# A decode attention kernel's output projection: four column tiles with an fp32 sum, and two of A's wo rows a partition loaded apart on 32 partitions

## The chip, the core and the metric

The kernel runs on one core of one Trainium2 chip. A core has TensorE (PE; its weight loads are listed as PEld), VectorE (DVE), ScalarE (ACT), GpSimd (POOL), and SyncE (SP), which here only issues DMAs; 16 DMA engines carry the transfers between HBM and the on-chip memory SBUF. Matmuls write to PSUM, which has banks of 512 fp32 columns. The metric is the device time of one execution in microseconds, as the median of several runs.

## What is computed

Two independent single-token attention layers, A and B, whose output rows are put side by side:

```python
# for A; B is the same with the last W = 4096 keys of its cache
B, Sq, D = 1, 1, 512;  Hq, Hkv, Sk, Dh = 32, 32, 16384, 128
q = (x @ wq).reshape(B, Sq, Hq, Dh).transpose(0, 2, 1, 3)
scores = einsum("bhqd,bhkd->bhqk", q, k_cache) * Dh ** -0.5
p = softmax(scores)
o = einsum("bhqk,bhkd->bhqd", p, v_cache)
row = o.transpose(0, 2, 1, 3).reshape(B, Sq, Hq * Dh) @ wo      # wo: 4096 x 512
out = concatenate([row_A, row_B], axis=-1)                       # 1 x 1 x 1024, bf16
```

All inputs are bf16. A's caches are 128 MB each for K and V, of B's the last quarter is read (32 MB each), and each wo is 4 MB.

## The kernel before

**The main loop.** The work is cut into 20 loads, 16 of A (two heads each) and 4 of B (eight heads each, as two units), one of B after every four of A; the last load is B's. A load is a K tile and a V tile of 128 partitions x 256 keys x 128. For each load, DVE multiplies K by the query (`_mult`, L169) and adds the halves (`_add`, L178); TensorE sums the rest with an identity (`_red`, L190) into the PSUM tile `red`; DVE reduces that to scores (L206) and ScalarE takes the exponential (L212), a load later than the multiplication. `_pv` (L231) multiplies the probabilities with V, with the matmuls spread over four column tiles of TensorE (output rows 0, 32, 64 and 96 in turn, `r = 32 * (t % 4)`); `_fin_pick` (L245, L251) and `_fin_fold` (L259) gather the head's rows into `f_ps`.

**Buffers and the order of DMAs.** K tiles take turns in two buffers (pool `kt`), V tiles have one (pool `vt`). `_Loads` holds a list of transfers with the pool that each needs; `release` frees a slot when the last reader of a tile has been issued, and `pump` then issues what is next in the list, so the order on SP's queue is the list's. The last V tile goes into the `kt` slot of the K tile before the last. After it comes wo, in the one `vt` slot: A's in two pieces of 16 rows a partition, B's in five of 16, 8, 4, 2 and 2 rows a partition (`_load_wo`, L146). wo lies in SBUF with 32 rows a partition, `src = st.wo.rearrange("(p j) f -> p j f", j=J)`, J = 32, so a piece is one run of 16, 8, 4 or 2 KB in each of the 128 partitions.

**The end.** `_fin_rows` sums the exponentials with one fp32 matmul for A and one for B (L270), normalizes (L276, L278) into `orow` (head x 128) and moves `orow` with four small matmuls a layer (L287) to the layout of wo, 128 partitions x 32 columns. `_out` is called once for each piece of wo in the order of the transfers: it copies that tile to bf16 (L300) and multiplies one column of it with one row a partition of wo at a time (L307), 1 x 512 for A (32 matmuls into one PSUM row) and two of 1 x 256 in two column tiles for B (64 matmuls). With the last piece the row is cast to bf16 (L316, L318) and written out by a DMA from SP (L319). The two result rows share one buffer (pool `accs`).

Everything in `_out`, `_fin_rows` and the loads is kept in program order on each engine by `cx.o`.

Of the kernel before, what the change touches and what calls it, by code (L numbers as in the profile page):

```python
# [8 lines left out]
F32 = mybir.dt.float32  # L9
BF16 = mybir.dt.bfloat16  # L10
P = 128
# [3 lines left out]

DH = 128
W = 8
KEYS = 256
SCALE = 1.0 / math.sqrt(DH)

# [119 lines left out]
def _load_wo(nc, cx, st, j0, n):  # L140
    J = st.wo.shape[0] // P
    if cx.wo_t is None:
        cx.wo_t = cx.vt_pool.tile([P, 2, J, st.DN], BF16, tag="vt", name="wo_t")
    src = st.wo.rearrange("(p j) f -> p j f", j=J)
    st.wo_t = cx.wo_t[:, st.at // st.DN, :, :]
    cx.o(nc.sync.dma_start(out=st.wo_t[:, j0 : j0 + n, :], in_=src[:, j0 : j0 + n, :]))  # L146


def _load_kv(nc, cx, load, which, tag):
    pool = cx.kt_pool if tag == "kt" else cx.vt_pool  # L150
    t = pool.tile([P, KEYS, DH], BF16, tag=tag, name=which)
    setattr(load, which, t)
    load.v_tag = tag
    st = load.st
    view = st.k_view if which == "kt" else st.v_view
    for u in load.units:
        src = view[u.h0 : u.h0 + u.R].rearrange("g (i l) d -> i g l d", l=st.keys)
        cx.o(nc.sync.dma_start(out=t[:, u.k0 : u.k0 + st.keys, :], in_=src))
# [42 lines left out]
def _softmax(nc, cx, load):  # L201

    st = load.st
    R = st.R
    sc = cx.sc_pool.tile([P, KEYS], F32, tag="sc", name="sc")
    cx.o(nc.vector.tensor_reduce(out=sc[:, :], in_=load.red[:, :, :], axis=AX.X, op=ALU.add))  # L206
    for u in load.units:
        n = st.keys
        u.p = cx.p_pool.tile([P, n // 4, R, 4], BF16, tag="p", name="p_sb")
        for g in range(R):  # L210
            h = st.f_at + u.h0 + g
            cx.o(nc.scalar.activation(  # L212
                out=u.p[:, :, g, :],
                in_=sc[:, u.k0 : u.k0 + n].rearrange("p (t e) -> p t e", e=4),
                func=ACT.Exp,
                scale=SCALE,
                bias=st.off[:, g : g + 1],
                accum_out=cx.cs[:, h : h + 1],
            ))
# [46 lines left out]

def _fin_rows(nc, cx, sts):
    H = 32
    for st in sts:
        cx.o(nc.tensor.matmul(  # L270
            cx.f_ps[st.f_at : st.f_at + H, DH : DH + 1],
            lhsT=cx.cs[:, st.f_at : st.f_at + H], rhs=cx.ones_col[:, 0:1],
            start=False, stop=True, skip_group_check=True,
        ))
    recip = cx.small.tile([2 * H, 1], F32, tag="recip", name="recip")
    cx.o(nc.vector.reciprocal(recip[:, :], cx.f_ps[0 : 2 * H, DH : DH + 1]))  # L276
    orow = cx.small.tile([2 * H, DH], BF16, tag="orow", name="orow")
    cx.o(nc.scalar.activation(  # L278
        out=orow[:, :], in_=cx.f_ps[0 : 2 * H, 0:DH], func=ACT.Copy, scale=recip[:, 0:1]
    ))  # L280
    for st in sts:
        J = st.wo.shape[0] // P
        n = DH // J
        h = st.f_at
        for r in range(n):
            at = cx.place_at + n * h - r
            cx.o(nc.tensor.matmul(  # L287
                st.oc_ps[:, 0:J],
                lhsT=cx.place[h : h + H, at : at + P],
                rhs=orow[h : h + H, r * J : (r + 1) * J],  # L290
                start=(r == 0), stop=(r == n - 1),
                skip_group_check=True,
            ))


def _out(nc, cx, st, j0, n):
    J = st.wo.shape[0] // P
    if j0 == 0:
        st.oc = cx.singles.tile([P, J], BF16, tag=f"oc{st.name}", name=f"oc{st.name}")
        cx.o(nc.vector.tensor_copy(st.oc[:, :], st.oc_ps[:, 0:J]))  # L300
    if cx.out_ps is None:
        cx.out_ps = cx.red_pool.tile([P, 2, 512], F32, tag="red", name="out_ps")
    w = st.DN // st.cols
    out = [cx.out_ps[r : r + 1, b, 0:w] for r, b in st.out_at]
    for j in range(j0, j0 + n):
        for x in range(st.cols):
            cx.o(nc.tensor.matmul(  # L307
                out[x],
                lhsT=st.oc[:, j : j + 1],
                rhs=st.wo_t[:, j, x * w : (x + 1) * w],  # L310
                start=(j == 0),
                stop=(j == J - 1),
            ))
    if j0 + n == J:
        row = cx.accs_pool.tile([1, st.DN], BF16, tag="accs", name=f"row{st.name}")
        cx.o(nc.vector.tensor_copy(row[0:1, 0:w], out[0]))  # L316
        if st.cols == 2:
            cx.o(nc.scalar.copy(row[0:1, w:], out[1]))  # L318
        cx.o(nc.sync.dma_start(out=cx.out[0, 0:1, st.at : st.at + st.DN], in_=row[0:1, :]))  # L319
# [3 lines left out]
def kernel(  # L323
# [14 lines left out]
    nc = tc.nc  # L338
# [4 lines left out]
    cx = _Ctx()  # L343
# [18 lines left out]
    ld = cx.loads = _Loads({"kt": 1, "vt": 1})  # L362
    cx.scr = cx.kt_pool.tile([P, KEYS * DH], BF16, tag="kt", name="scr")
    cx.wo_t = None

    def problem(name, x, k_cache, v_cache, wq, wo, sk0, W, at):
        st = _Problem()
        st.name, st.x, st.wq, st.wo, st.at = name, x, wq, wo, at
        st.R, st.keys = (2, KEYS) if name == "A" else (4, KEYS // 2)
        assert st.R * W == P * st.keys  # L370
        st.DN = wo.shape[1]
        st.k_view = k_cache[0, :, sk0 : sk0 + W, :]
        st.v_view = v_cache[0, :, sk0 : sk0 + W, :]
        st.out_at = ((0, 0),) if name == "A" else ((64, 0), (96, 1))
        st.cols = len(st.out_at)
        st.f_at = 0 if name == "A" else 32
        assert k_cache.shape[1] == 32
        n = KEYS // st.keys * st.R
        st.loads = [_Load(st, i) for i in range(k_cache.shape[1] // n)]
        st.units = [u for x in st.loads for u in x.units]  # L380
        return st

    stA = problem("A", A_x, A_k_cache, A_v_cache, A_wq, A_wo, 0, SkA, 0)
# [14 lines left out]
            ld.add("vt", lambda x=loads[i - 1]: _load_kv(nc, cx, x, "vt", "vt"))  # L398
    ld.add("kt", lambda x=loads[-1]: _load_kv(nc, cx, x, "vt", "kt"))
    J = A_wo.shape[0] // P  # L400
    pieces = [(stA, 0, J // 2), (stA, J // 2, J // 2)]
    j0 = 0
    for x in (J // 2, J // 4, J // 8, J // 16, J // 16):
        pieces.append((stB, j0, x))
        j0 += x
    for i, p in enumerate(pieces):
        ld.add(None if i else "vt", lambda p=p: _load_wo(nc, cx, *p))

    ld.pump()

# [2 lines left out]
    at = (stA.R + stB.R) * (A_wq.shape[0] // P) * P  # L413
# [9 lines left out]
        out=cx.ident[:, :],  # L423
        in_=ones[:, 0:P],
# [9 lines left out]
    w = cx.place_at + 2 * P  # L434
    cx.place = cx.singles.tile([64, w], BF16, tag="place", name="place")
    nc.gpsimd.affine_select(
        out=cx.place[:, :],
        in_=ones[0:64, 0:w],
# [4 lines left out]
        channel_multiplier=-n_r,  # L443
    )

    cx.cs = cx.singles.tile([P, 64], F32, tag="cs", name="cs")
    rows = cx.small.tile([P, 32], F32, tag="rows", name="rows")
    nc.vector.tensor_reduce(
        out=rows[:, :], in_=cx.ident[:, :].rearrange("p (c w) -> p w c", w=32), axis=AX.X, op=ALU.add,
    )  # L450
    for st in (stA, stB):
        H, R = 32, st.R
# [30 lines left out]
    cx.f_ps = cx.psf_pool.tile([P, 512], F32, tag="f", name="f_ps")  # L483
    stA.oc_ps = cx.pst_pool.tile([P, 512], F32, tag="ocp", name="oc_ps")
    stB.oc_ps = cx.acc[1]
    cx.out_ps = None

    _spread_x(nc, cx, stA, 0, 0)
    _spread_x(nc, cx, stB, 1, stA.R * (A_wq.shape[0] // P) * P)
# [12 lines left out]
    for i, x in enumerate(loads):  # L502
# [11 lines left out]
            end(prev)  # L514
        prev = x
    _softmax(nc, cx, prev)
    for u in prev.units:
        _pv(nc, cx, u)
    end(prev)
# [33 lines left out]
```

The softmax here doesn't subtract the row's maximum and nothing guards it: scores larger than these inputs give would overflow.

## Time and profile before

| what | value |
|---|---|
| median of 4 runs | 823.15 us (822.99 to 823.37) |
| the profiled execution's own time | 823.08 us |
| its span, first to last instruction | 821.4 us |
| mean granted TensorE clock | 0.697 of full |
| DMA | 352.63 MB, mean 429 GB/s over the span |
| busy: DVE / PE / PEld / ACT / POOL | 600.7 / 301.0 / 117.2 / 35.1 / 1.3 us |
| chain that ended last, by engine | DMA 61%, issue 15%, DVE 13%, PE 11% |

All times within a profile are microseconds from the span's start. In tables of groups a line gives the kernel's line, the engine, the operation and the tile, out<-in, with the number of instructions, and in brackets the idle time of the engine before it with what ended it. "DMA" and "GB/s" are the mean busy share of the 16 DMA engines and what they moved. "q1" is the queue row of SP's transfers, "q8" that of instruction fetches, in packets of 16 KB. PEclk is the granted share of the full TensorE clock.

### The profile page before, as it was taken

How to read it: one execution, taken by the hardware profiler on the slowest of the kernel's cores; microseconds unless marked ns; L12 is line 12 of the kernel's file. 1: busy time of each engine (PE TensorE's matmuls, PEld its weight loads, DVE VectorE, ACT ScalarE, POOL GpSimd, SP SyncE). 2: the span in 40 equal slices, each digit the busy share in tenths (PEclk: the TensorE clock that was granted, in tenths of full speed). 3: DMA queues.
4: the chain of work that ended last, by engine and by line, in shares of the span. 5: the costliest groups of instructions: out<-in, count | busy, mean ns of one | idle time of the engine just before them, and what ended most of it. 6: DMA issues, size and time to landing. Idle time of an engine off the chain costs nothing.

```text
span 821.4 us, 4767 instructions
## 1 busy us (share of the span) xinstructions
PE 301.0 (37%) x2148; PEld 117.2 (14%) x2148; DVE 600.7 (73%) x146; ACT 35.1 (4%) x133; POOL 1.3 (0%) x9
## 2 busy tenths in 40 slices
PE   3423705143333415060606151423414250606087
PEld 1211202011111102020202020101101020202033
DVE  2099895996496867799196949599659677689921
ACT  0100000000010000000001000000001000000010
POOL 0000000000000000000000000000000000000000
PEclk9855769585757667686858595857666675758589
DMA  9999999999999999999999999999999999999997
GB/s 385 436 457 412 453 415 451 412 454 418 429 440 447 422 444 426 440 417 448 419 444 437 434 432 437 428 424 441 444 415 451 424 448 418 451 412 450 415 426 317
DMA packets 8236, 352.63 MB, mean 429 GB/s; under 512 B 916, under 2 KB 920, under 8 KB 1304
## 3 DMA queue, kind: packets, MB, share of 16 engines
q1 hardware_dynamic: 8212, 352.33, 99.3%
q8 instruction: 17, 0.28, 0.1%
q14 instruction: 3, 0.02, 0.0%
q10 hardware_dynamic: 4, 0.00, 0.0%
HBM read 352.32 MB, written 0.00 MB: 429 GB/s over the span
## 4 chain that ended last, share of the span: by engine, by line
DMA 61%; issue 15%; DVE 13%; PE 11%; ACT 0%; SPq 0%; DVEq 0%
DMA kt<-in_A_k_cache_dram 42%; DMA vt<-in_A_v_cache_dram 12%; PE red L190 7%; DVE kt L178 6%; DVE kt L169 4%; PE acc L231 4%; DMA vt<-in_B_v_cache_dram 4%; DMA wo_t<-in_B_wo_dram 4%; DVE sc L206 2%; ACT p_sb L212 0%; SPq L115 0%; PE out_ps L307 0%; DVE rowB L316 0%; DVEq L169 0%
## 5 line engine op out<-in xcount | busy, mean ns | idle before, releaser
L169 DVE TENSOR_TENSOR kt<-kt,qallA 128x32768 bf16<-128x32768 bf16 (+2 forms) x20 | 276.2, 13810 | 161.9 <-DMA kt<-in_A_k_cache_dram 161.9
L231 PE MATMUL acc<-vt,p_sb 128*8 128x512 bf16 (+1 forms) x1280 | 113.3, 531 | 443.4 <-ACT p_sb L212 344.1
L178 DVE TENSOR_TENSOR kt<-kt 128x16384 bf16<-128x16384 bf16 (+2 forms) x24 | 174.3, 7262 | 0.2
L190 PE MATMUL red<-kt,ident 128*128 128x512 bf16 x640 | 149.9, 393 | 56.3 <-DVE kt L178 56.3
L231 PEld LDWEIGHTS <-p_sb 128*8 128x8 bf16 (+1 forms) x1280 | 37.7, 112 | 514.9 <-ACT p_sb L212 419.3
L190 PEld LDWEIGHTS <-ident 128*128 128x128 bf16 x640 | 62.6, 100 | 143.0 <-issue 45.3
L169 DVE TENSOR_TENSOR kt<-kt,qallB 128x16384 bf16<-128x16384 bf16 x8 | 69.5, 8686 | 2.7 <-DMA kt<-in_B_k_cache_dram 2.7
L206 DVE TENSOR_REDUCE sc<-red 128x256 f32<-128x2048 f32 x20 | 45.7, 2284 | 5.6 <-PE red L190 5.6
L212 ACT ACTIVATE p_sb<-sc,offA 128x256 bf16<-128x256 f32 x32 | 16.0, 500 | 573.6 <-DVE sc L206 573.6
L245 DVE TENSOR_TENSOR acc<-acc,maskA 128x512 f32<-128x512 f32 x16 | 11.1, 695 | 22.1 <-PE acc L231 22.1
L130 PE MATMUL q_ps<-wq_t,scr 128*128 128x512 bf16 x64 | 17.1, 434 | 6.9 <-DMA wq_t<-in_A_wq_dram 5.0
L212 ACT ACTIVATE p_sb<-sc,offB 128x128 bf16<-128x128 f32 x32 | 12.4, 388 | 160.8 <-DVE sc L206 160.8
L251 DVE TENSOR_REDUCE s<-acc 128x128 f32<-128x512 f32 x24 | 16.6, 692 | 0.8
L245 DVE TENSOR_TENSOR acc<-acc,maskB 128x512 f32<-128x512 f32 x8 | 5.5, 693 | 5.7 <-PE acc L231 5.7
L130 PEld LDWEIGHTS <-scr 128*128 128x128 bf16 x64 | 6.9, 108 | 16.7 <-issue 11.2
L307 PE MATMUL out_ps<-wo_t,ocA 128*1 128x512 bf16 x32 | 8.4, 429 | 0.2 <-DVE ocA L300 0.2
L316 DVE CAST rowA<-out_ps 1x512 bf16<-1x512 f32 x1 | 0.7, 678 | 8.5 <-PE out_ps L307 8.5
L259 PE MATMUL f_ps<-s,selA 128*32 128x128 f32 x32 | 6.5, 285 | 0.0
L212 ACT ACTIVATION_READ_ACCUMULATOR p_sb<-sc,offA 128x1 f32 x32 | 6.0, 187 | 0.0
L212 ACT ACTIVATION_READ_ACCUMULATOR p_sb<-sc,offB 128x1 f32 x32 | 6.0, 186 | 0.0
L102 DVE CAST scr<-xT 128x128 bf16<-128x128 f32 (+1 forms) x6 | 2.1, 460 | 3.6 <-PE xT L94 3.5
L307 PE MATMUL out_ps<-wo_t,ocB 128*1 128x256 bf16 x64 | 4.1, 272 | 1.3 <-DVE ocB L300 0.9
(43 smaller groups left out, 26.4 us busy)
## 6 DMA issues: line engine op xcount, KB each, us to landing
kt<-in_B_k_cache_dram SPq DMA_DIRECT2D x8, 4096.0 KB, 32.8
vt<-in_B_v_cache_dram SPq DMA_DIRECT2D x8, 4096.0 KB, 23.1
wq_t<-in_A_wq_dram SPq DMA_DIRECT2D x1, 4096.0 KB, 12.2
wq_t<-in_B_wq_dram SPq DMA_DIRECT2D x1, 4096.0 KB
wo_t<-in_A_wo_dram SPq DMA_DIRECT2D x2, 2048.0 KB, 22.9
wo_t<-in_B_wo_dram SPq DMA_DIRECT2D x1, 2048.0 KB, 27.3
wo_t<-in_B_wo_dram SPq DMA_DIRECT2D x1, 1024.0 KB, 29.3
wo_t<-in_B_wo_dram SPq DMA_DIRECT2D x1, 512.0 KB
```

Of the source, the lines that this page charges most:

```text
L102: cx.o(nc.vector.tensor_copy(st.xb[:, :, g, :].rearrange("p c (i r) -> p r c i", r=R)[:, g, :, :], xT[:, :].rearrange("p (c o) -> p c o", ...
L130: cx.o(nc.tensor.matmul(q_ps[:, j, :], lhsT=st.xb[:, c, g, :], rhs=w[:, g, j * (512 // DH) : (j + 1) * (512 // DH), :], start=(g == 0 and ...
L169: cx.o(nc.vector.tensor_tensor(out=k, in0=k, in1=q.rearrange("p (o d) -> p o d", o=1).broadcast_to([P, b - a, DH]), op=ALU.mult,))
L178: cx.o(nc.vector.tensor_tensor(out=k[:, :, 0 : DH // 2], in0=k[:, :, 0 : DH // 2], in1=k[:, :, DH // 2 : DH], op=ALU.add,))
L190: cx.o(nc.tensor.matmul(load.red[:, k : k + n, :], lhsT=cx.ident[:, :], rhs=load.kt[:, k : k + n, b * W : (b + 1) * W], start=(b == 0), st ...
L206: cx.o(nc.vector.tensor_reduce(out=sc[:, :], in_=load.red[:, :, :], axis=AX.X, op=ALU.add))
L212: cx.o(nc.scalar.activation(out=u.p[:, :, g, :], in_=sc[:, u.k0 : u.k0 + n].rearrange("p (t e) -> p t e", e=4), func=ACT.Exp, scale=SCALE, ...
L231: cx.o(nc.tensor.matmul(u.acc[r : r + 4 * R, :], lhsT=u.p[:, t, :, :], rhs=u.load.vt[:, k : k + 4, :], start=(t < 4), stop=(t >= T - 4),))
L245: cx.o(nc.vector.tensor_tensor(out=acc, in0=acc, in1=st.mask[:, :].rearrange("p (x o) -> p x o", o=1).broadcast_to([P, 4, DH]), op=ALU.mult,))
L251: cx.o(nc.vector.tensor_reduce(out=u.s[:, :], in_=acc.rearrange("p x d -> p d x"), axis=AX.X, op=ALU.add,))
L259: cx.o(nc.tensor.matmul(cx.f_ps[st.f_at : st.f_at + 32, 0:DH], lhsT=st.sel[:, at : at + 32], rhs=u.s[:, :], start=(u.i == 0), stop=(u.i == ...
L307: cx.o(nc.tensor.matmul(out[x], lhsT=st.oc[:, j : j + 1], rhs=st.wo_t[:, j, x * w : (x + 1) * w], start=(j == 0), stop=(j == J - 1),))
```

## The change

1. A's wo piece of the last rows has 14 rows a partition instead of 16 (`APART = 2`). The two rows left out of each partition, 256 KB, are loaded by `_load_apart` into a tile `more` in the `kt` pool: one partition a head (a block), with 4 x 2 rows of 512 in it, heads 0 to 19 on partitions 0 to 19 and heads 20 to 31 on partitions 32 to 43. Each of its eight DMAs takes every fourth partition, five blocks in the first four DMAs and three in the last four. The first four stand in the list after A's first piece of wo, the last four after A's second. GpSimd sets partitions 0 to 31 of the tile to zero before the first of them.
2. A small matmul with `spread` (a selection of the identity) and a copy bring the values of `orow` that belong to those rows to the same partitions (`oc_x`); they give eight more matmuls of 44 partitions.
3. All of A's matmuls of `_out` (16 + 8 + 14) and B's first 16 (now 1 x 512) go to four column tiles in turn, in one PSUM bank for each layer, which DVE sets to zero after the last softmax. DVE then copies the bank to SBUF as fp32 (`sums`), and an fp32 matmul with a column of ones adds its rows up: for A into a row of another bank, for B into the two 1 x 256 rows after the next eight wo rows a partition (`sum_at` 24).
4. The sums of the exponentials of A and B are one fp32 matmul instead of two, and the bf16 copies of both layers' tiles move from `_out` to `_fin_rows`.

```diff
+APART = 2
+def _load_apart(nc, cx, st, part):
+    J = st.wo.shape[0] // P
+    H = st.wo.shape[0] // DH
+    n = DH // J
+    if part == 0:
+        more = cx.kt_pool.tile([P, KEYS, DH], BF16, tag="kt", name="more").rearrange("p k d -> p (k d)")
+        at = n * APART * st.DN
+        cx.wo_x = more[:, 0:at].rearrange("p (r j f) -> p r j f", r=n, j=APART)
+        cx.sums = more[:, at : at + 2048].bitcast(F32).rearrange("p (b f) -> p b f", b=2)
+        cx.o(nc.gpsimd.memset(cx.wo_x[0:32], 0.0))
+    src = st.wo.rearrange("(h r j) f -> h r j f", h=H, j=J)
+    h0, to, k = ((0, 0, 5), (20, 32, 3))[part]
+    for a in range(4):
+        cx.o(nc.sync.dma_start(
+            out=cx.wo_x[to + a : to + a + 4 * k - 3 : 4],
+            in_=src[h0 + a : h0 + a + 4 * k - 3 : 4, :, J - APART : J, :],
+        ))
 def _fin_rows(nc, cx, sts):
-    for st in sts:
-        cx.o(nc.tensor.matmul(
-            cx.f_ps[st.f_at : st.f_at + H, DH : DH + 1],
-            lhsT=cx.cs[:, st.f_at : st.f_at + H], rhs=cx.ones_col[:, 0:1], ...
+    cx.o(nc.tensor.matmul(
+        cx.f_ps[0 : 2 * H, DH : DH + 1], lhsT=cx.cs[:, :], rhs=cx.ones_col[:, 0:1], ...
...
+        if st.apart:
+            moved = cx.out_ps[0:64, 3, 0 : n * st.apart]
+            cx.o(nc.tensor.matmul(
+                moved, lhsT=cx.spread[:, :],
+                rhs=orow[h : h + H, :].rearrange("p (r j) -> p r j", j=J)[:, :, J - st.apart : J], ...
+            st.oc_x = cx.small.tile([64, n * st.apart], BF16, tag="oc_x", name="oc_x")
+            cx.o(nc.vector.tensor_copy(st.oc_x[:, :], moved))
...
+        st.oc = cx.singles.tile([P, J], BF16, tag=f"oc{st.name}", name=f"oc{st.name}")
+        cx.o(nc.vector.tensor_copy(st.oc[:, :], st.oc_ps[:, 0:J]))
 def _out(nc, cx, st, j0, n):
...
-    for j in range(j0, j0 + n):
+    todo = [(st.oc[:, j : j + 1], st.wo_t[:, j, :]) for j in range(j0, j0 + n)]
+    if st.apart and j0 == 0:
+        todo += [
+            (st.oc_x[0:44, i : i + 1], cx.wo_x[0:44, i // st.apart, i % st.apart, :])
+            for i in range(DH // J * st.apart)
+        ]
+    last = j0 + n == J - st.apart
+    if j0 < st.parts:
+        for i, (oc, wo) in enumerate(todo):
+            r = 32 * (i % 4)
+            cx.o(nc.tensor.matmul(
+                cx.out_ps[r : r + 1, st.bank, :], lhsT=oc, rhs=wo, ...
+        if j0 + n == st.parts:
+            cx.o(nc.vector.tensor_copy(cx.sums[:, st.bank, :], cx.out_ps[:, st.bank, :]))
+        todo = []
+    for i, (oc, wo) in enumerate(todo):
         for x in range(st.cols):
             cx.o(nc.tensor.matmul(
-                out[x], lhsT=st.oc[:, j : j + 1], rhs=st.wo_t[:, j, x * w : (x + 1) * w], ...
+                out[x], lhsT=oc, rhs=wo[:, x * w : (x + 1) * w], ...
+    if j0 + n == st.sum_at:
+        for x in range(st.cols):
+            cx.o(nc.tensor.matmul(
+                out[x], lhsT=cx.ones_col[:, 0:1], rhs=cx.sums[:, st.bank, x * w : (x + 1) * w], ...
-    if j0 + n == J:
+    if last:
...
-        st.out_at = ((0, 0),) if name == "A" else ((64, 0), (96, 1))
+        st.out_at = ((0, 2),) if name == "A" else ((64, 0), (96, 3))
+        st.apart = APART if name == "A" else 0
+        st.bank, st.parts, st.sum_at = (0, 32 - APART, 32 - APART) if name == "A" else (1, 16, 24)
...
-    pieces = [(stA, 0, J // 2), (stA, J // 2, J // 2)]
+    pieces = [(stA, 0, J // 2), (stA, J // 2, J // 2 - APART)]
...
         ld.add(None if i else "vt", lambda p=p: _load_wo(nc, cx, *p))
+        if i < 2:
+            ld.add(None if i else "kt", lambda i=i: _load_apart(nc, cx, stA, i))
...
+    cx.spread = cx.singles.tile([32, 64], BF16, tag="spread", name="spread")
+    nc.vector.memset(cx.spread[:, :], 0.0)
+    nc.vector.tensor_copy(cx.spread[:, 0:20], cx.ident[0:32, 0:20])
+    nc.vector.tensor_copy(cx.spread[:, 32:44], cx.ident[0:32, 20:32])
...
     _softmax(nc, cx, prev)
+    cx.out_ps = cx.red_pool.tile([P, 4, 512], F32, tag="red", name="out_ps")
+    cx.o(nc.vector.memset(cx.out_ps[:, 0:2, :], 0.0))
```

## The prediction, made before the changed kernel had run

> **What bounds the kernel now.** I read the page first: the DMA row and the queues.
>
> ```profile
> DMA  9999999999999999999999999999999999999997
> ...
> q1 hardware_dynamic: 8212, 352.33, 99.3%
> q8 instruction: 17, 0.28, 0.1%
> ```
>
> The 16 DMA engines are busy in every slice but the last: the kernel is a stream of 352 MB, and nothing in the diff changes how many bytes are read. Only the tail can move, so next comes the chain that ended last, in order of time (start us, us, what):
>
> ```profile
> 789.17 29.14 DMA wo_t<-in_B_wo_dram
> 818.31 0.04 issue
> 818.35 0.43 PE out_ps L307 x4
> 818.78 0.41 DVE rowB L316
> ```
>
> The last 256 KB of B's wo lands at 818.31, four matmuls and a cast follow, then the row's DMA. The third view is the busy time by stage over the tail, whose last two columns are the DMA share and GB/s:
>
> ```profile
> 814.00:815.00 1.00, 0.85 (x16) 0.70 (x18) 0.09 (x1) 0.00 (x0) 0.00 (x0) 1.00 0.94 380
> 815.00:816.00 1.00, 1.00 (x22) 0.79 (x18) 0.00 (x0) 0.00 (x0) 0.00 (x0) 1.00 0.58 236
> 816.00:817.00 1.00, 0.93 (x18) 0.61 (x13) 0.00 (x0) 0.00 (x0) 0.00 (x0) 1.00 0.50 197
> 817.00:818.00 1.00, 0.88 (x12) 0.51 (x12) 0.00 (x0) 0.00 (x0) 0.00 (x0) 1.00 0.34 131
> ```
>
> From 815 on only half of the engines still work. The semaphore events of the trace say it exactly: the last piece lands in 16 parts, eight at 815.05 to 815.94, eight at 817.79 to 818.31. The spread of one DMA's parts was 0.7 us at 41 us and 2.1 us right after the first instruction packet of q8 (at 60.7 us); 16 such packets, 0.88 us or more each, came before the end, which fits eight engines that took two each. So the eight late engines set the end, and the early eight have 1.9 to 3.3 us to spare. The fourth view is TensorE's order in the tail:
>
> ```profile
> 804.87 8.41 PE L307 MATMUL out_ps<-wo_t,ocA 128*1 128x512 bf16 x32 [0.24 <-DVE ocA L300]
> 814.15 2.78 PE L307 MATMUL out_ps<-wo_t,ocB 128*1 128x256 bf16 x48 [0.87 <-DVE ocB L300]
> 817.12 0.98 PE L307 MATMUL out_ps<-wo_t,ocB 128*1 128x256 bf16 x12 [0.19 <-DMA wo_t<-in_B_wo_dram]
> 818.35 0.38 PE L307 MATMUL out_ps<-wo_t,ocB 128*1 128x256 bf16 x4 [0.26 <-DMA wo_t<-in_B_wo_dram]
> ```
>
> It waits 0.19 and 0.26 us for data: it is nearly late itself, so an earlier landing is worth something only if TensorE's work shrinks too. The diff does both.
>
> **Part 1, the bytes.** A's second wo piece falls from 16 to 14 rows a partition: 16 KB less on each of 16 engines. A piece of 128 KB an engine takes 4.84 us (A's two pieces land at 803.66 and 808.50), so 16 KB is 0.61 us, off the late eight: last landing 818.31 - 0.61 = 817.70.
>
> The moved 256 KB goes out as four DMAs of five blocks and four of three, a block being 8 KB in four packets of 2 KB. I take one engine a block, the first five: 64 KB on three engines, 32 KB on two. B's last piece (eight 2 KB packets an engine) lands 0.63 us after the one before it, 0.079 a packet; 32 packets are 2.5 us, net of part 1 +1.9 us. Early engines at 815.05 to 815.94 become 816.95 to 817.85, about the new last landing. That the first engine is an early one is shown: rowA's DMA of one partition, queued behind that engine's wo packets, landed at 815.23. For the other four I have no row; the bounds are all 256 KB on one engine (128 packets, 10.1 us) and an even spread (nothing gained). I take five early engines, since rowA's is one and the early set is half of all.
>
> The Trainium skill (DMA: Bandwidth & Descriptors, "Why a DMA increments its semaphore by 16 and not by 1") says that a DMA of five partitions runs on the five lowest-numbered engines and one of three on three; no row of before shows it. The same page's "Rules for kernel authors" speaks against the change: it advises against transfers under 64 KB as mostly overhead. The row above disagrees for packets behind others in a queue: 2 KB packets cost 39 ns a KB, the large ones 38. With the page's 2.0 us a DMA ("Anatomy of one DMA"), one after another, an estimate would be 16 us on the early engines and a kernel some 13 us slower.
>
> **Part 2, the queue on SP.** In the order that the changed program builds to, SP issues A's first piece, four small DMAs, A's 14 rows, four small ones, B's five. The first small one waits for GpSimd's memset of 32x4096, which waits for the last red (792.2). GpSimd's 128x384 memset took 0.417 us, so by elements 4.4: 796.7. Four issues at up to 0.43 each, and A's 14 rows stand in the queue at 798.8; the early engines run dry of A's first piece at 800.4, the late ones at 803. Covered; if the memset took twice that, the early half would idle 3 us and the late half not.
>
> Eight completion semaphores go round, so each DMA waits for the one eight places before. The sixth small one waits for B's last V load (798.82), the seventh for A's first piece (803.66); behind it stand the eighth and B's first pieces, issued from about 804.5 at 0.43 each. The three early engines without extra load idle 1.0 to 1.5 us there, inside their spare; the late ones have work until 807.4. B's fourth piece waits for A's 14 rows (807.9) and is needed after 813. Price nothing.
>
> rowB's cast waits for rowA's DMA (one buffer), which now ends behind the first engine's extra packets: 815.23 + 1.9 = 817.1, before the cast at 818.1. Covered by 1.0.
>
> **Part 3, TensorE.** Four column tiles: the pv matmuls of the same shape run four in 0.216 us at full and in 0.427 at half clock (their weight loads come four every 0.43). A's first 16 take 0.9 to 1.7 from 805.1, done by 806.8. Then TensorE waits for the eighth small DMA (on the early engines 800.4 to 801.2, + 1.25 + 4.24 + 1.25 = 807.1 to 807.9) and A's 14 rows (807.9): 22 matmuls, 1.3 to 2.6, to 810.5 at the latest. The sums copy is a 128x512 f32 row like L245's, 0.70. The fp32 fold: a fold of 128 columns shows as two records 0.107 apart at full clock, four times bf16, so 512 columns cost 0.85 or 1.7: done at 810.7 to 813. B's first piece lands at 813.35 - 0.61 = 812.74; at worst 0.3 late.
>
> B's first 16: 0.9 or 1.7; their copy with the hops 0.95, for which the next matmul waits: 814.6 or 815.6, against the second piece at 815.23. 16 matmuls of 256 in pairs: 0.85 or 1.7. Two folds: 0.43 side by side at full clock, up to 1.7 one after another at half. The last 16 need 0.85 at full clock, gated at 816.47, 817.07 and 817.70. At full clock the fold ends at 816.5 to 817.0 and the last landing still ends the chain: **-0.6 us**. At half clock the fold ends at 818.2 to 819.0 and the last four start at 818.9 to 819.7 instead of 818.35: **+0.5 to +1.4 us**.
>
> Which clock? Busy time by stage, cut where the clock changed (PE busy is the second number, PEclk the third from the end):
>
> ```profile
> 800.80:804.21 3.41, 1.55 (x24) 0.87 (x17) 1.55 (x3) 0.31 (x1) 0.00 (x0) 1.00 1.02 432
> 804.21:807.63 3.42, 3.07 (x15) 1.05 (x15) 0.19 (x1) 0.06 (x1) 0.00 (x0) 0.50 1.00 426
> 811.04:814.45 3.41, 2.54 (x17) 0.93 (x17) 0.78 (x2) 0.00 (x0) 0.00 (x0) 1.00 0.98 410
> 814.45:817.87 3.42, 3.23 (x58) 2.31 (x54) 0.00 (x0) 0.00 (x0) 0.00 (x0) 1.00 0.55 220
> ```
>
> After a stage with 1.55 of 3.41 us busy the clock was halved; after 2.54 it stayed. Over all stages, with each matmul's drain of 0.16 us taken off, it fell only under 0.38 busy and rose only over 0.75. The changed TensorE is busy for 1.3 to 2.5 us of a stage between 804 and 815: near the lower edge, so where the stages happen to be cut decides. Working the tail through for evenly spaced cuts, some 6 in 10 keep full clock; the median of runs then goes with them.
>
> The Trainium skill (TensorE: Matmul & The Clock Gate, "What's actually happening") has the clock fall only after an idle window of about 3.4 us; by that the waits here, all under 2 us, would never halve it, and the estimate is -0.6 without the other case. The rows say that less idling is enough.
>
> **Edits hidden in any case.** The memset of two PSUM banks (L482's rows: two of 0.485) lies in DVE's 4.4 us idle before 799.0. Three small DVE operations for spread fall into the set-up, where DVE waits for the first K. One spread matmul (0.18) and oc_x's copy (0.17) delay A by 0.2, ahead of a wait for data. One f_ps matmul less is under 0.1. TensorE has 16 instructions fewer of 4215: no packet of q8 moves before the tail.
>
> **The rivals.** Forecast (0.50): 823.08 - 0.6 = 822.5, and 0.07 for the median over the profiled run: 822.6, between 822.2 and 822.9.
>
> TensorE late at half clock (0.22): 823.6 to 824.6, decided by a stage under 0.38 busy before 815. For: the row above. Against: the waits that are cut short at half clock.
>
> Slower: one of the three engines with 64 KB is a late one (0.15). Its landing goes to 818.31 + 1.9 = 820.2 and the kernel to 825.0; it decides as soon as one late engine stands among the first three (with one of the 32 KB pair alone it is +0.6). For: only the first engine's side is seen. Against: eight of sixteen behave alike, which a run of neighbours explains as well.
>
> The change does not do what it says: the small DMAs spread over all engines (0.05), 822.9 to 824.0; or all lie on one (0.03): 814.8 + 10.1 - 0.6 = 824.3 against 818.0 for its last packet, 829.4. A gain that I don't see (0.05): under 821.5.
>
> **The numbers.** 0.2% of 823.15 is 1.65 us, about what a measurement of this kernel can tell from no change. Slower by more: 0.12 of the engines' case, 0.03 of the half clock's, 0.03 of the single engine's, 0.18. Faster by more: 0.05. Within: 0.77. The range 822.1 to 824.7 takes the forecast, nearly all of the half clock's case and the even spread, and leaves some 0.2 out.
>
> **What would show it.** Right: the last piece's late parts land at 817.7, the early at up to 817.8, and the DMA share stays above 0.8 until 817; the last four matmuls still wait for DMA. Wrong: parts of the last piece after 818.3 (engines), or no wait for DMA before the last matmuls with PEclk 0.50 after 814 (clock).

## The result, and the profile after

| | before | after |
|---|---|---|
| median of all runs | 823.23 us (65 runs, 822.80 to 824.55) | 824.97 us (43 runs, 822.50 to 826.90) |
| ratio after / before | | 1.0016, 95% interval 1.0012 to 1.0021 |
| profiled execution: own time, span | 823.08, 821.4 | 823.26, 821.4 |
| last part of wo lands at | 818.31 | 818.36 |

The change makes the kernel slower, by 1.74 us in the medians. (The ratio is that of the means; that of the medians is 1.0021, because the times fall in groups.) The times of the changed kernel are spread much wider than those before: 15 of 43 lie at 822.5 to 823.8, 22 at 824.1 to 825.9, six at 826.3 to 826.9. The spans, from the first to the last instruction, say the same without the 1.7 to 3.0 us that an execution takes outside its span: their median is 823.1 us over 44 executions, where the kernel before had 821.1 to 822.4 in the executions run beside the experiments, with a median of 821.3. Only five of the 44 are shorter than 821.1. The profiled execution is one of the short ones, so its page alone can't show what the median lost. It does show whether the parts of the change work.

The tail by stages (span, then busy time of PE, PEld, DVE, ACT and POOL, PEclk, DMA share, GB/s), from the changed kernel's profile:

```profile
814.00:815.00 1.00, 1.00 (x16) 0.16 (x4) 0.34 (x1) 0.00 (x0) 0.00 (x0) 0.50 0.95 393
815.00:816.00 1.00, 0.33 (x4) 0.08 (x1) 0.61 (x1) 0.00 (x0) 0.00 (x0) 0.81 0.98 395
816.00:817.00 1.00, 0.86 (x16) 0.70 (x17) 0.09 (x1) 0.00 (x0) 0.00 (x0) 1.00 1.03 396
817.00:818.00 1.00, 1.00 (x20) 0.63 (x15) 0.00 (x0) 0.00 (x0) 0.00 (x0) 1.00 0.19 70
```

The DMA share after 815 was 0.58, 0.50 and 0.34; now it is 0.98, 1.03 and 0.19. The moved rows do run on engines that had time to spare, and the transfers now end nearly together, but for one engine. By the packets' records of the trace 15 engines finish at 816.8 to 817.5, and one at 818.07. That one engine sets the last landing. Next, the chain of waits (start us, us, what):

```profile
799.64 8.32 DMA wo_t<-in_A_wo_dram
...
808.34 10.02 DMA wo_t<-in_B_wo_dram
818.36 0.04 issue
818.40 0.43 PE out_ps L349 x4
818.83 0.41 DVE rowB L361
```

In this execution the end still hangs on a DMA, 0.05 later than before. The timeline of the tail (start us, us, engine, line, operation; in brackets the idle time before it and what ended it) shows both queues that the prediction followed:

```profile
792.78 3.50 POOL L160 MEMSET more<- 32x4096 bf16 x1 [790.78 <-PE red L211]
796.31 3.28 SPq L164 DMA_DIRECT2D more<-in_A_wo_dram  x4
799.64 0.45 SPq L147 DMA_DIRECT2D wo_t<-in_A_wo_dram  x1
800.13 5.06 SPq L164 DMA_DIRECT2D more<-in_A_wo_dram  x4
805.24 3.54 SPq L147 DMA_DIRECT2D wo_t<-in_B_wo_dram  x5
808.15 1.02 PE L340 MATMUL out_ps<-more,oc_x 44*1 44x512 bf16 x8 [2.84 <-DMA more<-in_A_wo_dram]
809.10 1.87 PE L340 MATMUL out_ps<-wo_t,ocA 128*1 128x512 bf16 x14
811.76 1.87 PE L355 MATMUL out_ps<-more,ones_col 128*1 128x512 f32 x2 [0.79 <-DVE more L345]
813.43 1.91 PE L340 MATMUL out_ps<-wo_t,ocB 128*1 128x512 bf16 x16
816.14 1.04 PE L349 MATMUL out_ps<-wo_t,ocB 128*1 128x256 bf16 x16 [0.81 <-DVE more L345]
```

On SP (SPq) the order is the predicted one, and the stretch of small DMAs is longer: four issues take 3.28 us. On PE, A's 14 and B's first 16 tile matmuls run at half clock (1.87, 1.91), and the clock comes back at 815.38, just in time for B's second piece (1.04 for 16 matmuls). Two questions follow: what happens when the clock does not come back, and why one engine is 0.6 us behind the rest.

### The profile page after: what moved, and what is told of

Same layout as the page of the kernel before. It is cut to its first block, busy times and chain, and to the rows that moved or that the text cites. A ratio compares the mean times of both kernels' runs of the same rounds, so it can differ in the third digit from the quotient of the medians.

```text
span 821.4 us, 4782 instructions
## 1 busy us (share of the span) xinstructions
PE 295.0 (36%) x2143; PEld 113.8 (14%) x2143; DVE 603.4 (73%) x153; ACT 35.1 (4%) x133; POOL 4.8 (1%) x10
## 4 chain that ended last, share of the span: by engine, by line
DMA 59%; issue 15%; PE 12%; DVE 12%; ACT 1%; SPq 1%; POOLq 0%; DVEq 0%
DMA kt<-in_A_k_cache_dram 42%; DMA vt<-in_A_v_cache_dram 15%; PE red L211 7%; PE acc L252 6%; DVE kt L199 5%; DVE kt L190 4%; DVE sc L227 2%; DMA wo_t<-in_B_wo_dram 1%; DMA wo_t<-in_A_wo_dram 1%; ACT p_sb L233 1%; POOLq L602 0%; SPq L164 0%; SPq L116 0%; PE out_ps L349 0%; DVE rowB L361 0%
## 5 line engine op out<-in xcount | busy, mean ns | idle before, releaser
L252 PE MATMUL acc<-vt,p_sb 128*8 128x512 bf16 (+1 forms) x1280 | 109.5, 517 | 444.0 <-ACT p_sb L233 344.4
L160 POOL MEMSET more<- 32x4096 bf16 x1 | 3.5, 3502 | 790.8 <-PE red L211 790.8
```

Source lines behind the costliest of these rows:

```text
L160: cx.o(nc.gpsimd.memset(cx.wo_x[0:32], 0.0))
L252: cx.o(nc.tensor.matmul(u.acc[r : r + 4 * R, :], lhsT=u.p[:, t, :, :], rhs=u.load.vt[:, k : k + 4, :], start=(t < 4), stop=(t >= T - 4),))
```

## The experiments

The theories. CLOCK: TensorE falls to half clock between 804 and 812, and where it stays there to the end, TensorE is late. DRY: small DMAs and the memset keep A's 14 rows and B's first piece back on SP's queue; the early engines run dry, the packets after that are slow, and one engine ends late. The rival of both is the prediction's: the small packets lie on a late engine.

"Extra time" below is worked out from the packets' records after 780: the sum, over all packets, of what each took beyond what most of its size take (0.611 us for 16 KB, 0.534 for 14 KB, 0.084 for 2 KB). Before the change it is 1.0 us, in the changed kernel's profile 7.3. The sums move by up to 0.7 us, in `eight` by 2, with how small excesses are counted; no reading below hangs on that.

### The changed kernel again: three more profiles

No edit.

> The changed kernel once more, for a second profiled execution and more times. Its times lay from 822.5 to 826.9 in three groups near 823.1, 825.0 and 826.7, where the kernel before stays within 822.8 to 824.6. Theory CLOCK: the groups differ by whole clock stages of 3.4 us at half clock, 1.7 us of work each, so a profile of a long execution (span over 822.5) shows PEclk 0.50 after 815.4 and last matmuls that wait for no DMA. Theory DMA: a long execution shows the last piece of B's wo landing later than 818.4, by as much as the span is longer, and last matmuls that wait for it.

> The changed kernel, for the profile of a long execution. CLOCK, if its span is over 822.5: PEclk 0.50 past 815.4 and last matmuls that wait for no DMA, last landing under 818.4. DMA or DRY: last landing over 818.4 and last matmuls that wait for it.

> The changed kernel, for the profile of a long execution. CLOCK, if its span is over 822.5: PEclk 0.50 past 815.4 and last matmuls that wait for no DMA, last landing under 818.4. DMA or DRY: last landing over 818.4 and last matmuls that wait for it.

`again`: 823.68 us (822.78 to 826.01), ratio 1.0011 (1.0002 to 1.0020). The other two are a pair that shows the matter best: 825.70 and 823.10 us, spans 823.6 and 820.9, while the last part of wo lands at 818.05 and 817.83. DMA differs by 0.2, the end by 2.7. Stages of 3.41 us, cut where the clock may change, first `again2`, the long one:

```profile
804.08:807.50 3.42, 1.40 (x25) 0.46 (x24) 0.45 (x3) 0.31 (x1) 0.00 (x0) 1.00 0.96 375
810.91:814.33 3.42, 2.63 (x19) 0.65 (x17) 0.92 (x2) 0.00 (x0) 0.00 (x0) 0.50 0.99 419
814.33:817.74 3.41, 2.60 (x22) 1.04 (x16) 1.14 (x2) 0.00 (x0) 0.00 (x0) 0.50 0.82 325
817.74:821.15 3.41, 3.27 (x28) 1.46 (x22) 0.11 (x1) 0.08 (x1) 0.00 (x0) 0.50 0.02 5
```

and `again3`, the short one:

```profile
811.16:814.57 3.41, 2.75 (x17) 0.96 (x18) 1.29 (x2) 0.00 (x0) 0.00 (x0) 0.50 0.97 410
814.57:817.99 3.42, 2.61 (x41) 1.56 (x36) 0.69 (x1) 0.00 (x0) 0.00 (x0) 1.00 0.74 291
```

The same work is cut differently. With 2.75 busy in the stage before 814.57 the clock rises; with 2.63 and then 2.60 it does not, and the whole end runs at 0.50. The chain of `again2`:

```profile
816.58 1.87 PE out_ps L349 x16
818.45 0.85 PE out_ps L355 x4
819.30 1.75 PE out_ps L349 x16
821.05 0.41 DVE rowB L361
```

There is no DMA in it after 808.21; TensorE alone ends it, at 821.05 where a landing at 817.7 and four matmuls were meant. In `again3` the same three rows take 1.04, 0.43 and 0.97. CLOCK is shown as the difference between these two executions. `again` shows the fall and the rise:

```profile
805.33:808.74 3.41, 1.91 (x33) 0.59 (x32) 0.45 (x3) 0.35 (x1) 0.00 (x0) 1.00 1.02 408
812.16:815.57 3.41, 2.83 (x18) 0.86 (x17) 1.19 (x2) 0.00 (x0) 0.00 (x0) 0.50 0.99 412
```

Its clock is 0.50 from 808.74 to 815.57 and 1.00 after that. Its span is 820.8, 0.6 under that of the profile before.

### The tiles without the moved rows

```diff
-APART = 2
+APART = 0        # and no small DMAs, no memset
```

> Parts 3 and 4 of the change alone: four column tiles and the fp32 sums, with A's wo in two whole pieces as before. CLOCK: the sparse work of TensorE is there, so times spread over 2 us or more and the median lies at 823.5 to 825.5. DMA: the transfers are those of before, so the times are those of before, 822.8 to 823.8, as the early engines keep their lead and the last piece lands at 818.3.

823.89 us, ratio 1.0011 (1.0002 to 1.0020), and two groups of times: five at 823.15 to 823.44, five at 824.34 to 825.21. The transfers are those of before (last landing 818.36). So the two groups do not need the small DMAs: the column tiles bring them alone. In the profiled execution, one of the short ones, the stage after A's first piece is nearly empty,

```profile
805.05:808.46 3.41, 0.10 (x4) 0.00 (x0) 0.00 (x0) 0.00 (x0) 0.00 (x0) 0.50 0.99 423
```

since 16 matmuls that took some 4 us in one PSUM row take 1 us in four tiles. Faster matmuls made TensorE idle. That the long group is the one whose clock stays down is argued from `again2`; no execution of that group was profiled here.

### The moved rows without the tiles

```diff
-        st.bank, st.parts, st.sum_at = (0, 32 - APART, 32 - APART) if name == "A" else (1, 16, 24)
+        st.bank, st.parts, st.sum_at = 0, 0, -1
...
-    cx.o(nc.vector.memset(cx.out_ps[:, 0:2, :], 0.0))
```

> Parts 1 and 2 of the change alone: the eight small DMAs, with TensorE's matmuls for A and B one after another as before (38 of 1x512 and 64 of 1x256, no fp32 sums). CLOCK: TensorE is dense from 804 to 817 but starts A's last 22 matmuls only at 808, ends them at 812.9 and has the same 64 matmuls for B behind them, so the time is 823.0 to 823.5 with a spread under 1 us. DMA: the spread of 4 us and the median near 825 stay.

823.19 us (822.40 to 825.04), ratio 1.000 (0.9991 to 1.0010). Four of ten runs, 822.40 to 822.87, have the gain that was forecast. In the profiled execution, 823.87, the clock is 1.00 from 808.13 to the end, and two engines are late:

```profile
817.00:818.00 1.00, 0.81 (x18) 0.52 (x14) 0.00 (x0) 0.00 (x0) 0.00 (x0) 1.00 0.29 102
818.00:819.00 1.00, 0.86 (x12) 0.41 (x9) 0.00 (x0) 0.00 (x0) 0.00 (x0) 1.00 0.07 27
```

0.07 of 16 engines over the last stage is about one engine's work. One engine's last part lands at 819.09, another's at 818.62, all others by 817.8. So a second fault remains with the clock out of the way.

### Holding the clock with filler matmuls

```diff
+def _fill(nc, cx, st, n):          # n matmuls whose results are not used
+    for i in range(n):
+        cx.o(nc.tensor.matmul(cx.f_ps[0:1, :], lhsT=st.oc[:, i : i + 1], rhs=st.wo_t[:, i, :], ...
```

8 stand before the moved rows' matmuls, 3 after each copy to `sums`, 5 after A's fold.

> The changed kernel with 19 matmuls of 1x512 more, whose results nobody reads: 8 ahead of the wait for the small DMAs, 3 after each copy to the sums is issued, 5 after A's fold. They fill TensorE's waits, so that its clock stays full. CLOCK: the groups at 825 and 826.7 go, the median is 822.5 to 823.3. DMA: the times stay spread to 826 with a median near 825.

> The kernel warm once more, beside seven_warm on the same chip and for more times: 822.6 to 824.1 again, median 823.0 to 823.2. If this profile shows a longer time than 823.0, one engine's last packets must be late by as much (landing after 818.2) with PEclk at 1.00; if the clock is 0.50 after 808 in it, the fillers do not hold the clock and the verdict on the clock weakens.

`warm`: 823.10 us (822.59 to 824.11), ratio 0.9999 (0.9989 to 1.0008), beside 823.68 for the unfilled kernel on the same chip. The profile has PEclk 1.00 from 799.35 to the end of the work, and the end is the forecast one to 0.04 us:

```profile
808.28 9.46 DMA wo_t<-in_B_wo_dram
817.74 0.04 issue
817.78 0.43 PE out_ps L360 x4
```

`warm2`: 823.72 (822.62 to 825.05), ratio 1.0005 (0.9997 to 1.0014). Its profile has full clock from 808.29 and one engine late (last landing 818.57, the others by 817.9), extra time 9.0 us. The fillers remove the times above 825.1 (16 of 43 in the changed kernel and 3 of 10 in `again`, none of 21 here), which supports CLOCK. The times of 823.7 to 825.05 that are left, with this profile and that of `apart_only`, show that the late engine is a fault of its own. Holding the clock brings the kernel back to the time before, not to the forecast.

### Eight blocks a DMA

```diff
-    h0, to, k = ((0, 0, 5), (20, 32, 3))[part]
-    for a in range(4):
...
+    for a in range(0, H, 8):       # no hole, so no memset and no `spread`; 32 KB on each of eight engines
+        cx.o(nc.sync.dma_start(out=cx.wo_x[a : a + 8], in_=src[a : a + 8, :, J - APART : J, :]))
```

> The same without the 16 extra matmuls: TensorE as sparse as in the change. CLOCK: landings as in the kernel with extra matmuls, but times spread from 822.4 to 825 or more with a median 0.5 to 2 us higher. If only the DMAs make the long runs: times as with the extra matmuls, 822.4 to 822.9.

> The 256 KB of A's apart rows in four DMAs of eight blocks (partitions 0 to 31, no zeroed gap, so no memset and no matmul and copy with the selection) right after A's first piece, and 16 matmuls of 1x512 more in TensorE's waits (8 ahead of A's second piece, 3 after each copy, 5 after A's fold; nobody reads them). Theory DRY: in the changed kernel early engines run dry near 800.5 and 806 because SP issues late, and start again with packets that take twice as long, which makes one engine late by 0.6 to 1.4 us in some executions. Here SP issues A's 14 rows at 796 and B's first piece at 799, no engine runs dry: early parts of the last piece at 815.7 to 816.6, late ones at 817.7, and with the clock kept full 822.4 to 822.9 in nearly all runs. If the slow packets have another cause: a last part at 818.3 or later in some runs, times up to 824.

`eight`: 826.85 us, ratio 1.0043 (1.0031 to 1.0056); with fillers 825.58, 1.0029 (1.0018 to 1.0041). The expected 822.4 to 822.9 was missed by some 3 us. The last part lands at 820.04 and 820.62. All eight parts of a small DMA show six early and two late engines, so two late ones get 32 KB more. And while these DMAs run every engine is slow: the 2 KB packets take 0.111 us in the mean instead of 0.084, 14 and 16 KB packets up to 0.45 us more, extra time 19.1 us. Several things had been changed at once: the number of blocks, their place on neighbouring partitions, and the order, with all the small DMAs ahead of A's 14 rows. The next kernel changes only the place.

```diff
-    for a in range(0, H, 8):
-        cx.o(nc.sync.dma_start(out=cx.wo_x[a : a + 8], in_=src[a : a + 8, ...
+    for a in range(4):             # eight_apart: the same eight blocks on every fourth partition
+        cx.o(nc.sync.dma_start(out=cx.wo_x[a : a + 29 : 4], in_=src[a : a + 29 : 4, ...
```

> The kernel eight with the eight blocks of a DMA on every fourth partition (heads a, a+4, ... a+28 for a of 0 to 3) instead of on eight neighbouring partitions; engines, bytes and issues are the same, 32 KB on each of the eight lowest engines, two of them late ones. Theory, writes to neighbouring partitions slow the packets: the mean of a 2 KB packet falls from 0.111 us to about 0.084 and the extra time of slow packets from 19 to 25 us to some 7; the two late engines still carry 32 - 16 KB more, so the last landing is 818.31 + 0.64 = 818.95, and the time 823.8 at full clock, up to 825.5 at half. Rival, the number of engines that write small packets slows them: the mean stays at 0.10 or more, the last landing at 819.8 or later, the time 825.6 to 827.2 as for eight.

824.79 us (823.34 to 825.57), ratio 1.0013 (1.0003 to 1.0022). The 2 KB packets take 0.084 us, none more; the extra time is 0.9 us; the last part lands at 818.61 (expected 818.95). The place is what slowed them; it cost 1.4 us of the last landing. (In HBM the blocks of a DMA lie as far apart as their heads, so their distance there changed in the same step; no run parts the two.) Two late engines end behind the others because they carry more, and no other engine is late: A's 14 rows went out at 794.32 and B's first piece at 794.81, before any queue was empty, so this is a first sign for DRY, with the whole 256 KB. The rest is TensorE: PEclk is 0.50 from 805.84 to 819.49.

`seven_warm` lays heads 0 to 31 on partitions 0 to 31 without a hole, by DMAs of five blocks six partitions apart, with fillers:

```diff
+    for a in range(4) if part == 0 else range(4, 7):
+        k = 5 if a < 6 else 2
+        h = a if a < 6 else 30
+        e = h + 6 * k - 5 if a < 6 else 32
+        step = 6 if a < 6 else 1
+        cx.o(nc.sync.dma_start(out=cx.wo_x[h:e:step], in_=src[h:e:step, :, J - APART : J, :]))
```

> The kernel warm with the moved rows laid out without a hole: heads 0 to 31 on partitions 0 to 31, in seven DMAs (six of five blocks, a stride of six partitions apart, and one of two), so that GpSimd's memset, spread, its matmul and oc_x's copy are gone; A's 14 rows then stand in SP's queue some 3.5 us earlier (about 796 instead of 799.6), before the early engines run dry of A's first piece at 800.4. Engines 0 and 1 take 56 KB, 2 to 4 take 48 KB. Theory, running dry makes the slow first packets at 800 to 803 and with them the engine that is sometimes late: extra time of slow packets falls from some 7 us to under 4, last landing at 817.7 with every engine by 817.8, times within 822.3 to 822.7, median 822.5, ratio 0.9993 to the kernel before. Rival, the late engine has another cause: the last landing still lies between 817.7 and 819.1 from run to run and the times spread up to 824, as those of warm, median 823.0. With the fillers the clock does not come in.

824.72 us (824.40 to 825.37), ratio 1.0016 (1.0007 to 1.0025): a miss. The 2 KB packets take 0.116 us in the mean and the extra time is 30.5 us, a part of it behind a dry spell near 806.7, since B's first piece went out at 805.54 again; all engines are slowed, and the last part lands at 819.54. For the small packets a distance of six partitions is as bad as neighbours; a distance of four is free. The Trainium skill (DMA: Bandwidth & Descriptors, "The descriptor swizzle") has an engine write groups of four partitions in a transfer to all of them, partitions 0 to 3 by engine 0, 4 to 7 by engine 1. With blocks four apart, block i then falls on the partitions that engine i writes anyway, which agrees with 0.084 against 0.111 and 0.116 us; that two engines meeting on one group is the cause is argued from this, not shown, and the distance in HBM stays a rival.

### No dry queues

```diff
-        cx.o(nc.gpsimd.memset(cx.wo_x[0:32], 0.0))
-            (st.oc_x[0:44, i : i + 1], cx.wo_x[0:44, i // st.apart, i % st.apart, :])
-            for i in range(DH // J * st.apart)
+            (st.oc_x[a:b, i : i + 1], cx.wo_x[a:b, i // st.apart, i % st.apart, :])
+            for k in range(0, DH // J * st.apart, 2) for a, b in ((0, 20), (32, 44)) for i in (k, k + 1)
```

That is `early_warm` (fillers as in `warm`). In `never_dry` the last four small DMAs and their matmuls are left out as well, so A's row lacks what those 96 KB of wo would add.

> The kernel warm without GpSimd's memset: the matmuls of the moved rows are split into 20 partitions from 0 and 12 from 32 (16 instead of 8), so that the hole between them is never read. The small DMAs' partitions and engines stay as in the change. SP issues the first four small DMAs from 792.2 and A's 14 rows at 795.5 instead of 799.6, before the early engines run dry at 800.4; B's first piece still goes out at 805.2, so the second dry spell (806.2) stays. Theory, dry queues make the slow packets: those between 800 and 804 are gone and the extra time falls from 9.0 us (warm2) to some 3 to 4; the late engine comes less often or less late: median 822.6 to 823.0, none over 824.0. Rival, the late engine does not come from the first dry spell: median 823.1 to 823.7 as warm, with times up to 825.

> As early_warm, but the last four small DMAs and their matmuls are left out, so the two moved rows a partition of heads 20 to 31 (96 KB) are neither loaded nor counted in A's row. B's first piece then goes out at about 799 to 804 and no engine runs dry. Theory, dry queues make the late engine: extra time of slow packets under 1.5 us (one instruction packet's neighbour), last landing 817.70 within 0.15, times within 822.3 to 822.7, median 822.5, ratio 0.9992. Rival, the small packets themselves disturb the other engines: extra time of 3 us or more beside the four DMAs at 800 to 802, median 822.8 or more. Second rival, the engines that take the instruction packets differ from run to run: the last landing varies by 0.6 or more with hardly any slow packets.

`early_warm`: 824.04 us (823.88 to 825.60), ratio 1.0013 (1.0004 to 1.0022): a miss in the time, where 822.6 to 823.0 was expected. The slow packets of 800 to 804 are gone but for the one behind an instruction packet, and the extra time falls to 5.5 us, yet one engine is later than ever: its part of B's first piece lands at 814.59, the others by 812.75, and it keeps that distance to the end (819.68). Its first 16 KB packet started at 808.25 and took 1.51 us, the one after the next spell of empty queues.

`never_dry`: 822.38 us, 9 of 11 runs at 822.21 to 822.53, ratio 0.9991 (0.9982 to 1.0000). B's first piece goes out on SP before the queues run empty, the extra time is 1.0 us, and no engine is late:

```profile
804.29 13.23 DMA wo_t<-in_B_wo_dram
817.52 0.04 issue
817.56 0.43 PE out_ps L359 x4
```

The 96 KB that it leaves out belong to early engines; the late eight carry what they carry in the change. That leaves the question whether all 256 KB go without a late engine:

```diff
-        if i < 2:
+        if i < 3:      # after A's first piece, after A's 14 rows (one DMA), after B's first piece (three)
             ld.add(None if i else "kt", lambda i=i: _load_apart(nc, cx, stA, i))
```

with A's last eight matmuls, its copy and its fold beside B's first 16 (ahead of them in `reorder`, behind in `reorder_b`).

> All of the moved 256 KB again, as in early_warm, but issued in another order: A's first piece, the four DMAs of five blocks, A's 14 rows, one DMA of three blocks, B's first piece, the other three of three blocks, B's smaller pieces. B's first piece then goes out at about 799 instead of 805, so no engine runs dry. A's last eight matmuls (12 partitions), its copy and its fold stand beside B's first 16 matmuls, rowA has a buffer of its own, and 20 fillers hold the clock. Theory, dry queues make the late engine: extra time of slow packets under 2 us, last landing 817.5 to 817.8, times 822.2 to 822.7, median 822.4, ratio 0.9991 as in never_dry, now with the whole result. Rival, the second group of small packets disturbs wherever it stands: one engine late by 0.6 to 2 us in B's smaller pieces, median 823 to 824.5. Second rival, A's end now lies too late for TensorE: the last four matmuls start without a wait for DMA, 822.8 to 823.5.

> As reorder, with B's first 16 matmuls ahead of A's last eight and A's fold after B's copy. If the small DMAs of three blocks land after B's first piece, this order waits less; if before, it costs up to 0.4 us at the end. Same theories: 822.2 to 822.8 if nothing runs dry, 823 to 824.5 if the small packets disturb in any place.

All the small packets are there, each at 0.084 us; the extra time is 1.1 and 1.0 us; the last parts land at 817.61 and 817.78, and no engine stands out. For the slow packets DRY holds with the full transfer. For the late engine it rests on one profile of each kernel, since `warm` and `again` had none either, and on the 9 of 11 times of `never_dry`. The times are 824.82 (824.04 to 829.81), ratio 1.0034 (1.0018 to 1.0050), and 826.46 (823.70 to 827.63), 1.0033 (1.0022 to 1.0044): the second rival. Three of the eleven times of `reorder`, 829.22 to 829.81, are not explained. The chain of `reorder` has a DVE copy ahead of each PE step and no DMA after 814.65:

```profile
814.65 0.68 DVE more L386
815.34 0.04 issue
815.38 1.03 PE out_ps L347 x16
816.41 0.86 PE out_ps L357 x2
817.27 0.02 issue
817.30 0.70 DVE more L390
818.00 0.04 issue
818.04 1.04 PE out_ps L402 x16
```

The transfers gain 0.7 us and TensorE gives back more. No version with the whole result beats the kernel before.

## Why the prediction was wrong

**What was right.** The early half takes the moved rows: all five parts of each five-block DMA land on early engines (the first one's at 800.68 to 801.84). The late eight end 0.6 earlier: 817.73 in `again`, 817.74 in `warm`, against 817.70 predicted. The eighth small DMA landed at 807.8 to 808.2 (predicted 807.1 to 807.9). The 0.6 us can be had: the spans of `again`, `again3` and `warm`, in which no engine is late, are 820.8, 820.9 and 820.8 against 821.4, four runs of `apart_only` took 822.4 to 822.9, and `never_dry`, which does less, has a median of 822.38. The rival "one of the three engines with 64 KB is a late one" is refuted in its cause, and so are the even spread and the single engine; the prediction's estimate of 16 us from 2.0 us a DMA did not come either, for the eight small DMAs cost an early engine at most 32 packets of 0.084 us. (The section that it names is about DMAs issued from GpSimd; these are SyncE's.)

**The step that failed: the clock's share.** "Working the tail through for evenly spaced cuts, some 6 in 10 keep full clock; the median of runs then goes with them." In all four profiles of the changed kernel, and in `tiles_only`, the clock falls to 0.50 between 804 and 809: none of five keeps it. What saves the short ones is that it rises again by 814.57 to 815.57, before B's second piece. The question was not whether the clock falls but whether it comes back in time, and I had put the outcome on one evenly weighted cut of the stages, with edges (0.38 and 0.75 of a stage, drain taken off) read from a kernel with long runs of matmuls. Here it fell after a stage with 1.91 of 3.41 us busy (`again`, 805.33 to 808.74), in which the longest wait was 0.83 us; it rose after stages with 2.75, 2.83, 3.07 and 3.36, and not after 2.60 and 2.63, nor after one of 2.82 in `again3` of which 1.02 were the matmuls of 44 partitions. The changed work gives 2.6 to 3.4 in the deciding stage: it lies about the upper edge, where I had looked at the lower one. The edges themselves do not carry over either: the clock fell after stages with 2.27 us busy (`eight_apart`, 802.42 to 805.84) and 2.55 (`reorder`, 803.46 to 806.87), and did not rise after one with 2.84 (`eight`, 805.65 to 809.06). So the busy time of a stage does not decide alone; what else does stays open. What the prediction named as its refutation, no wait for DMA before the last matmuls with PEclk at 0.50 after 814, is what `again2` shows.

**Its size.** At half clock "+0.5 to +1.4". `again2` lost 2.6 over the profiled time before (825.70 - 823.08). Two terms were too small. The prediction has the last four matmuls start 0.7 us after B's fold, which is twelve matmuls at full clock; at half clock the last 16 take 1.75 us (0.97 at full), from 819.30, so the twelve take some 1.3. And it has B's second piece start by 815.6 at half clock; it started at 816.58, because the moved rows were there only at 808.21 (807.9 at the latest in the sum) and the 22 matmuls that waited for them took 2.84 us, from 808.59, where 2.6 was the bound.

**SP's queue, "Price nothing".** Two terms were off. The memset was quicker than estimated (3.50 for 4.4 us), a small DMA's issue dearer: 0.70 to 0.93 us each where 0.43 was the bound. A's 14 rows were issued at 799.64 (predicted 798.8) and B's first piece at 805.24 (804.5). Idle engines were counted, as "inside their spare"; what was not counted is that the packets after a dry spell are slow, 0.8 to 1.7 us for one of 14 KB that otherwise takes 0.534. And the spare was thin: the prediction itself put the engines with 64 KB at "816.95 to 817.85, about the new last landing". Nothing was left there for a stumble of 0.4 to 2.0 us. The cost is in the landing times, 818.05, 818.36, 818.57, 819.09, against 817.73 to 817.83 where no engine was late.

**The idle window.** The Trainium skill (TensorE: Matmul & The Clock Gate, "What's actually happening") has the clock fall after an idle window of about 3.4 us; the prediction weighed this against the trace and took the trace. `again` decides it: the clock fell after a window that was 0.56 busy.

**The chance of slower.** The rivals named both faults' kinds, but as one or the other. In the runs each appears without the other: the clock falls in `tiles_only`, which has no small DMA, and engines are late in `apart_only` and `warm2`, with full clock from 808.13 and 808.29 on. That the median falls where at least one of them acts is argued from this. The late engine shows in the profiles of the changed kernel, `again2`, `warm2` and `apart_only`, the clock that stays down in `again2`; how often each acts can't be told from the times alone.

**Still open.** Why only one or two engines are late after a dry spell, which ones, and why none is in `again`, `again3` and `warm`, whose queues ran dry as well; in `early_warm` its first packet of B's first piece started at 808.25, 0.69 us after the last small packet of any engine had ended, though the piece had been issued 3.2 us before.

## What to carry to other kernels

When work is taken off a busy engine to make room, look at what its clock makes of the idle time: a stage of 16 matmuls cut from some 4 us to 1 us let the clock fall, and in the execution where it had not come back before the last pieces the end was 2.7 us later than in one where it had. When a balance is made exact, the engines that end together have no spare left; price every spell in which a queue runs dry, and issue the transfer that keeps the queues full ahead of many small ones. Where a median falls between groups of times, forecast the share of executions in each group, since that is what decides.

## What the runs showed of the hardware

- Where a small DMA's blocks lie sets its speed and that of the transfers beside it: blocks four partitions apart 0.084 us for each 2 KB packet (`eight_apart`), neighbours 0.111 (`eight`), six apart 0.116 (`seven_warm`), with 0.9, 19.1 and 30.5 us of extra time in all packets, the last with a dry spell in it. The blocks' distance in HBM changed with that on the partitions.
- The first packets of an engine after its queue ran empty take up to three times as long: 1.74 us for 14 KB against 0.534 (`again`, at 800.70); with no dry spell (`never_dry`) none did but the one behind an instruction packet, 1.04.
- SP needs 0.70 to 0.93 us to issue a DMA of 20 or 12 short runs, more than the 0.33 to 0.45 us for one of 128 long runs (the changed kernel's profile).
- Four column tiles run 16 matmuls of 1 x 512 in 1.03 us at full clock and 1.9 at half (`again2`, the changed kernel), and their sums need a copy of 0.69 and an fp32 matmul of 0.86 (`reorder`) or, at half clock, 1.5 to 1.87 (`again2`); in the chains of `again2` and `reorder` nothing hides them.
